# Top-32 attention with a low-rank mixer: the later replacement rounds write their own tile

## The chip, the cores and the metric

The kernel runs on one core of a Trainium2 chip. The time is device microseconds, the median of three runs: 1773.88 us (1771.52 to 1775.6). A profile of one execution, with a span of 1773.6 us, is the source of everything below. The engines are TensorE (PE; its weight loads are shown apart as PEld), VectorE (DVE), ScalarE (ACT), GpSimd (POOL) and SyncE (SP), which issues the transfers here.

## The reference

```python
# attention: B, H, S, D = 8, 8, 576, 64, float32
scores = scale * np.matmul(q, k.transpose(0, 1, 3, 2))
kth = np.partition(scores, -32, axis=-1)[..., -32:-32 + 1]
scores = np.where(scores >= kth, scores, -1e9)
attn = softmax(scores)                       # with 1e-9 added to the sum
x = concat_heads(np.matmul(attn, v))         # (8, 576, 512)
# mixer: U (576, 32), V (32, 576), w_ch1 (512, 2048), w_ch2 (2048, 512)
h = x.transpose(0, 2, 1) @ U @ V
u = x + h.transpose(0, 2, 1)
out = u + np.maximum(u @ w_ch1, 0) @ w_ch2
```

For each of 8 x 8 x 576 rows of 576 scores the 32nd largest has to be found; all scores below it are dropped. That search is the part that the change touches.

## The kernel before, in words

**Tiling.** Heads are worked in pairs: 8 batches with four pairs each make 32 pairs. The 576 rows of a head are cut into four chunks of 128 and a rest of 64. A step `(g, t)` takes pair `g` and row chunk `t`. For `t` from 0 to 3 it holds two tiles of 128 x 576 scores, one for each head of the pair; in the code these two are `chunks[0]` and `chunks[1]`, and such a step is called a two-chunk step in this text. For `t = 4` the two rests of 64 rows share one tile: a one-chunk step. So there are 160 steps, 128 with two chunks and 32 with one.

**One step.** `scores` (L310) has TensorE compute the scores, and ScalarE copies them from PSUM to the tile `Ssb` (L344 to L346, L327). `front` (L366) finds the threshold. VectorE's MAX8 at L385 gives the eight largest of each row. Then come three rounds (`i` = 1, 2, 3): at L395 a replacement sets the eight values just found to -3e38, and at L399 MAX8 finds the next eight. After three rounds the smallest of the last eight is the 32nd largest. A replacement is two instructions in the trace: MATCH_VALUE_LOAD takes in the eight values, MATCH_REPLACE8 runs over the 576 elements. Within a round both chunks are replaced first (chunk 1, then chunk 0), and then both maxima are taken. After the rounds GpSimd (L402, L403) and ScalarE with GpSimd (L419 to L421) push the scores below the threshold down, and ScalarE takes the exponent with the row sum (L351). `turns` transposes the weights on TensorE, or `blocks` does so with a VectorE transpose (L446) and transfers (L452, L456). `values` multiplies with v (L498, L508, L512), `mixed` does the low-rank mixer, and `mlp` the two big products (L581, L600).

**Buffers of the rounds.** The first round reads `Ssb`, which is still needed, and so writes elsewhere: to a tile with the tag `rr`. The second and third round read an `rr` tile and write a new one. The tag has three buffers in rotation. Taking the next buffer makes its writer wait until the last reader of the old content is done. The waits are set by the framework from the tiles that instructions name, on the same engine too.

**Order.** On TensorE, ScalarE, VectorE and GpSimd the instructions run in the order in which the code names them. `front` is a generator that the main loop (L701 to L807) advances piece by piece between other work. `fill` (L673) puts in matmuls of the previous batch's `mlp` by a fixed share per step, so that they run beside the search of the next batch. Only the transfer queue on SyncE is ordered by the framework. Weights arrive in pairs of 32-bit words and are converted during the first two batches (L174 to L189, `next_params`), on ScalarE, VectorE and GpSimd. The two big products of the last batch come after all searches.

Of the kernel before, what the change touches and what calls it, by code (L numbers as in the profile page):

```python
# [8 lines left out]
F32 = mybir.dt.float32  # L9
# [17 lines left out]
def kernel(  # L27
# [29 lines left out]
    B, H, S, D = q.shape  # L57
    P = 128
# [24 lines left out]
    attn = ctx.enter_context(tc.tile_pool(name="attn", bufs=2))  # L83
# [265 lines left out]
    def weigh(chunk, E, nmax, total=None):  # L349

        nc.scalar.activation(E, chunk, AF.Exp, bias=nmax, scale=SCALE, accum_out=total)  # L351

    def ways(g, t):

        if (g, t) == (NPAIR - 1, NT - 1):
            return (0,), (), (1,)
        if (g, t) == (NPAIR - 1, NT):
            return (0,), (), ()  # L360
        return (), (1,) if t < NT else (), (0,)
# [4 lines left out]
    def front(g, t):  # L366

        if t == 0:
            dens[g] = small.tile([P, 2 * NT + 1], F32, tag="den", name="den", bufs=3)
        chunks, den = S2s.pop((g, t)), dens[g]
        n = len(chunks)
        E2 = attn.tile([P, 2 * S], F32, tag="E", name="E", bufs=3)
        Es = [E2[:, c * S : (c + 1) * S] for c in range(n)]
        sums = [den[:, 2 * t + c : 2 * t + c + 1] for c in range(n)]
        probs[g, t] = E2
        curs, ms = list(chunks), [None] * n
        first = small.tile([P, 2, 8], F32, tag="first", name="first", bufs=3)  # L380
        nmax = small.tile([P, 2], F32, tag="nmax", name="nmax", bufs=4)
        order = (1, 0) if n == 2 else (0,)
        for c in order:
            ms[c] = first[:, c]
            nc.vector.max(ms[c], curs[c])  # L385
        yield
        early, pooled, gaps = ways(g, t)
        for i in range(1, TOPK // 8):
            if i == 1:
                nc.scalar.mul(nmax[:, 0:n], first[:, 0:n, 0], -SCALE)  # L390
                for c in early:
                    weigh(chunks[c], Es[c], nmax[:, c : c + 1])
            for c in order:
                nxt = attn.tile([P, S], F32, tag="rr", name="rr", bufs=3)
                nc.vector.match_replace(nxt, ms[c], curs[c], NEG)  # L395
                curs[c] = nxt
            for c in order:
                ms[c] = small.tile([P, 8], F32, tag="m8", name="m8", bufs=8)
                nc.vector.max(ms[c], curs[c])  # L399
            yield  # L400
        for c in pooled:
            nc.gpsimd.tensor_scalar(Es[c], chunks[c], ms[c][:, 7:8], NEG, ALU.is_lt, ALU.mult)  # L402
            nc.gpsimd.tensor_tensor(chunks[c], chunks[c], Es[c], ALU.add)  # L403
        for c in early:
            nc.vector.scalar_tensor_tensor(
                out=Es[c],
                in0=chunks[c],
                scalar=ms[c][:, 7:8],
                in1=Es[c],
                op0=ALU.is_ge,  # L410
                op1=ALU.mult,
                accum_out=sums[c],
            )
        if t == NT:
            del qkTs[g]
        yield
        for c in gaps:
            least = small.tile([P, 1], F32, tag="least", name="least", bufs=3)
            nc.scalar.mul(least, ms[c][:, 7:8], WIDEN)  # L419
            nc.scalar.activation(Es[c], chunks[c], AF.Relu, bias=least, scale=-WIDEN)  # L420
            nc.gpsimd.tensor_tensor(chunks[c], chunks[c], Es[c], ALU.subtract)  # L421
            yield
        ahead = pooled if shared(g, t) else ()
        for c in ahead:
            weigh(chunks[c], Es[c], nmax[:, c : c + 1], sums[c])
            yield
        for c in order:
            if c not in early and c not in ahead:
                weigh(chunks[c], Es[c], nmax[:, c : c + 1], sums[c])
        if t == NT and g != NPAIR - 1:  # L430
            nc.scalar.activation(den, den, AF.Identity, bias=eps)
        yield

    def shared(g, t):


        return t < NT and g * CH + t >= ROUNDED
# [263 lines left out]
    for n in range(STEPS + 2):  # L701
        g, t = divmod(n, CH)
        if n < STEPS:
            if t == 0 and g + 1 < NP:
                load(g + 1)
            if t == 1 and g + 1 < NP:
                ready = prep(g + 1)
            fronts[n] = front(g, t)
            next(fronts[n])
# [131 lines left out]
```

## Time and profile before

| | busy, us | share of the span | instructions |
|---|---|---|---|
| TensorE, matmul | 1669.3 | 94% | 9851 |
| VectorE | 1560.3 | 88% | 3106 |
| ScalarE | 1029.4 | 58% | 2682 |
| GpSimd | 846.8 | 48% | 591 |

| group | count | mean, ns | busy, us |
|---|---|---|---|
| L385 MAX8 on `Ssb` | 288 | 742 | 203.3 |
| L395 replacement, `Ssb` to `rr` (round one) | 288 | 742 | 211.8 |
| L395 replacement, `rr` to `rr` (rounds two and three) | 576 | 742 | 427.2 |
| L399 MAX8 on `rr` | 864 | 748 | 614.7 |

How to read it. Times are in us from the start of the span unless marked ns. A group is one line and one operation; L395 is line 395 of the kernel. "Idle before, releaser" tells how long the engine stood still ahead of the group's instructions and what ended that. The chain of waits is followed back from the last instruction: at each step to what released it, or to the instruction before it on its engine; "issue" in it is time in which an engine waited for nothing that the profile shows. Two instructions of one engine can overlap in the record[...]. Busy time is then counted once.

### The profile page before, as it was taken

The page shows a single profiled execution, that of the slowest core. Times are in us where ns is not written, and L with a number is a line of the kernel's source. Part 1 is how long each engine was busy: PE and PEld are TensorE (multiplying, and loading weights), DVE is VectorE, ACT ScalarE, POOL GpSimd, SP SyncE. Part 2 cuts the span into 40 slices and gives each one's busy share as a digit, 9 for nine tenths or more (in the row PEclk, how much of TensorE's full clock was granted, in tenths as well). Part 3 has the DMA queues.
Part 4 walks back from the last instruction along what each step waited for, and adds up shares of the span by engine and source line. Part 5 has one row for each costly group of instructions (what it writes and reads, how often), then busy time and mean ns, then how long its engine had stood idle before and what let it go on. Part 6 is the DMA issues. An engine that isn't in the chain of part 4 may idle for free.

```text
span 1773.6 us, 28992 instructions
## 1 busy us (share of the span) xinstructions
PE 1669.3 (94%) x9851; PEld 1257.5 (71%) x9851; DVE 1560.3 (88%) x3106; ACT 1029.4 (58%) x2682; POOL 846.8 (48%) x591
## 2 busy tenths in 40 slices
PE   4666789999999999999999999999999999999999
PEld 2434556677777877788777877788777877788677
DVE  7999989899999999999999999999999999994000
ACT  4778777555656656565656656565656656564100
POOL 4777677535354554545445454444445444453000
PEclk7687799999999999999999999999999999999999
DMA  3222332222223332222233232232233232211010
GB/s 95 88 82 73 88 85 61 50 59 71 58 67 80 66 72 56 67 68 64 64 71 79 62 70 62 65 70 63 63 73 80 59 73 60 53 50 45 4 15 13
DMA packets 275829, 112.79 MB, mean 64 GB/s; under 512 B 173920, under 2 KB 260192, under 8 KB 275680
## 3 DMA queue, kind: packets, MB, share of 16 engines
q1 hardware_dynamic: 274624, 110.68, 26.4%
q8 instruction: 77, 1.26, 0.3%
q14 instruction: 72, 0.59, 0.1%
q10 hardware_dynamic: 1056, 0.26, 0.1%
HBM read 74.15 MB, written 36.70 MB: 63 GB/s over the span
## 4 chain that ended last, share of the span: by engine, by line
PE 75%; DVE 16%; POOL 4%; ACT 3%; issue 2%; DMA 1%; SPq 0%; POOLq 0%; DVEq 0%
PE mm L581 25%; PE mm L600 24%; DVE rr L395 7%; PE sc L333 6%; PE O L512 6%; DVE m L399 6%; PE tp L474 3%; DVE first L385 2%; PE sc L320 2%; PE O L498 2%; PE up L556 1%; PE O L508 1%; POOL E L402 1%; PE up L558 1%; PE tp L648 1%
## 5 line engine op out<-in xcount | busy, mean ns | idle before, releaser
L399 DVE MAX8 m<-rr 128x8 f32<-128x576 f32 x864 | 614.7, 748 | 5.5
L600 PE MATMUL mm<-hT,w 128*128 128x256 f32 (+1 forms) x2048 | 547.4, 410 | 0.0
L581 PE MATMUL mm<-uT,w 128*128 128x256 f32 (+1 forms) x2048 | 541.5, 410 | 0.9 <-ACT hT L593 0.9
L402 POOL TENSOR_SCALAR E<-Ssb,m 128x576 f32<-128x576 f32 x127 | 281.1, 2214 | 411.7 <-DVE m L399 409.1
L581 PEld LDWEIGHTS mm<-uT,w 128*128 128x128 f32 x2048 | 371.7, 190 | 115.1 <-issue 26.0
L600 PEld LDWEIGHTS mm<-hT,w 128*128 128x128 f32 x2048 | 368.3, 190 | 106.8 <-issue 22.5
L395 DVE MATCH_REPLACE8 rr<-m,rr 128x576 f32<-128x576 f32 x576 | 427.2, 742 | 0.0
L421 POOL TENSOR_TENSOR Ssb<-Ssb,E 128x576 f32<-128x576 f32 x159 | 225.4, 1418 | 122.3 <-ACT E L420 121.7
L351 ACT ACTIVATE E<-Ssb,nmax 128x576 f32<-128x576 f32 x288 | 223.3, 776 | 52.4 <-POOL Ssb L403 34.9
L593 ACT ACTIVATE hT<-mm 128x320 f32<-128x320 f32 (+1 forms) x256 | 105.1, 411 | 240.4 <-PE mm L581 240.1
L385 DVE MAX8 first<-Ssb 128x8 f32<-128x576 f32 x288 | 203.3, 742 | 31.4 <-ACT Ssb L346 31.4
L395 DVE MATCH_REPLACE8 rr<-first,Ssb 128x576 f32<-128x576 f32 x288 | 211.8, 742 | 0.0
L403 POOL TENSOR_TENSOR Ssb<-Ssb,E 128x576 f32<-128x576 f32 x127 | 179.3, 1412 | 10.6
L333 PE MATMUL sc<-qkT 64*128 64x288 f32 x1024 | 170.6, 454 | 6.7 <-ACT Ssb L344 5.8
L474 PE MATMUL tp<-ident,E 128*128 128x128 f32 x736 | 116.0, 283 | 37.1 <-ACT XT L521 14.6
L512 PE MATMUL O<-PT,va 128*64 128x128 f32 x2048 | 146.3, 284 | 1.9 <-DMA PT<-away 1.9
L474 PEld LDWEIGHTS tp<-ident,E 128*128 128x128 f32 x736 | 92.1, 145 | 68.7 <-ACT XT L521 16.6
L475 ACT COPY PT<-tp 128x512 f32<-128x512 f32 x184 | 106.6, 585 | 49.0 <-PE tp L474 46.4
L512 PEld LDWEIGHTS O<-PT,va 128*64 128x64 f32 x2048 | 113.7, 140 | 19.0 <-DMA PT<-away 2.9
L420 ACT ACTIVATE E<-Ssb,least 128x576 f32<-128x576 f32 x159 | 123.3, 776 | 5.2
L333 PEld LDWEIGHTS sc<-qkT 64*128 64x128 f32 x1024 | 93.3, 198 | 45.3 <-issue 14.3
L613 DVE TENSOR_TENSOR oT<-uT,mm 128x320 f32<-128x320 f32 (+1 forms) x8 | 3.6, 455 | 137.1 <-PE mm L600 137.1
(81 smaller groups left out, 1574.0 us busy)
## 6 DMA issues: line engine op xcount, KB each, us to landing
away<-y SPq DMA_DIRECT2D x416, 64.0 KB, 1.8
PT<-away SPq DMA_DIRECT2D x104, 256.0 KB, 2.8
raw<-in_moe_w_ch_dram SPq DMA_DIRECT2D x32, 512.0 KB, 3.8
va<-in_v_dram SPq DMA_DIRECT2D x64, 128.0 KB, 2.3
out_dram<-ob SPq DMA_DIRECT2D x57, 128.0 KB, 2.2
ld<-in_q_dram SPq DMA_DIRECT2D x108, 64.0 KB, 2.4
ld<-in_k_dram SPq DMA_DIRECT2D x108, 64.0 KB, 2.4
ld<-in_q_dram SPq DMA_DIRECT2D x108, 8.0 KB, 2.2
```

The lines of the kernel that those rows point to most:

```text
L333: nc.tensor.matmul(sc[:, h, 0:HALF], lhsT=qkT[half(h), 0, cols(t)], rhs=qkT[half(h), 1, i * HALF : (i + 1) * HALF], start=True, stop=True,)
L351: nc.scalar.activation(E, chunk, AF.Exp, bias=nmax, scale=SCALE, accum_out=total)
L385: nc.vector.max(ms[c], curs[c])
L395: nc.vector.match_replace(nxt, ms[c], curs[c], NEG)
L399: nc.vector.max(ms[c], curs[c])
L402: nc.gpsimd.tensor_scalar(Es[c], chunks[c], ms[c][:, 7:8], NEG, ALU.is_lt, ALU.mult)
L403: nc.gpsimd.tensor_tensor(chunks[c], chunks[c], Es[c], ALU.add)
L421: nc.gpsimd.tensor_tensor(chunks[c], chunks[c], Es[c], ALU.subtract)
L474: nc.tensor.transpose(tp[:, j, :], E2[:, a : a + P], ident)
L512: nc.tensor.matmul(O[half(h)], lhsT=va[:, h, j, :], rhs=PB[:, j] if h and shared(g, t) else PT[:, NT * h + j], start=False, stop=(j == NT ...
L581: nc.tensor.matmul(ph[:, 0:w], lhsT=w1[:, cc, f * P : (f + 1) * P], rhs=uT[:, cc, lo:hi], start=(cc == 0), stop=(cc == NC - 1),)
L600: nc.tensor.matmul(po[:, 0:w], lhsT=w2[:, f, c * P : (c + 1) * P], rhs=hTs[f][:, 0:w], start=(f == 0), stop=(f == NF - 1),)
```

## The change

The second and third round no longer take a new `rr` tile; they write into the tile that they read. The first round takes a tile as before. The tag keeps its three buffers; a two-chunk step now takes two of them instead of six. The purpose is to use fewer buffers, so that a replacement doesn't have to wait for a buffer to come free.

```diff
             for c in order:
-                nxt = attn.tile([P, S], F32, tag="rr", name="rr", bufs=3)
+
+                nxt = attn.tile([P, S], F32, tag="rr", name="rr", bufs=3) if i == 1 else curs[c]
                 nc.vector.match_replace(nxt, ms[c], curs[c], NEG)
                 curs[c] = nxt
```

The added empty line moves the numbers of all later lines up by one: L395 becomes L396, L399 becomes L400.

## The prediction

> **What bounds the kernel now.** I read the page by slices first, because an average over the span mixes a beginning and a long middle. The two rows to compare are TensorE (PE) and VectorE (DVE); I leave out the rows between and after them.
>
> ```profile
> PE   4666789999999999999999999999999999999999
> ...
> DVE  7999989899999999999999999999999999994000
> ```
>
> A slice is 44.3 us. TensorE is idle a third to a half of the first four slices and full from the seventh on; VectorE is full from the second slice to 1618 us and then has nothing to do. So there are at least three stages. The next view is the busy time of each engine in stretches; I cut it where the chain of waits (below) changes its engine.
>
> ```profile
> core 0: us, PE busy (x) PEld busy (x) DVE busy (x) ACT busy (x) POOL busy (x), PEclk, DMA share, GB/s
> 0.00:165.80 165.80, 95.10 (x586) 61.97 (x586) 154.36 (x316) 116.37 (x281) 110.32 (x95) 0.78 0.31 87
> 165.80:260.90 95.10, 78.11 (x443) 52.81 (x444) 89.53 (x183) 72.18 (x172) 69.06 (x48) 0.85 0.30 81
> 260.90:445.00 184.10, 173.29 (x1045) 130.71 (x1043) 173.18 (x346) 115.36 (x301) 101.69 (x71) 0.98 0.26 62
> 445.00:1618.00 1173.00, 1172.36 (x7115) 892.85 (x7114) 1135.65 (x2249) 703.15 (x1875) 561.13 (x373) 1.00 0.29 66
> 1618.00:1773.60 155.60, 150.48 (x669) 119.18 (x667) 7.52 (x17) 22.37 (x56) 4.63 (x5) 1.00 0.07 15
> ```
>
> The fourth line decides most. In 1173 us TensorE is idle 0.6 us and VectorE 37 us. The list of waits gives VectorE 17.4 us at L385 there, waiting for the score copy of L346, and gives TensorE no wait at all. A busy TensorE is not proof of a full one, so I looked at its pace. In the chain, 16 matmuls of 320 columns take 4.31 to 4.50 us (0.27 us each) and 20 of 256 columns take 4.32 us (0.216 us each). After 1645 us, where TensorE is alone, 128 of each take 34.45 and 27.63 us, so 0.269 and 0.216 us. It is the same pace: in the middle TensorE runs as fast as it ever does, and VectorE waits for it.
>
> The chain of waits says the same. Three pieces of it, from the beginning, from the middle and the last stretch (columns: start, duration, what):
>
> ```profile
> 63.43 0.74 DVE rr L395
> 64.17 0.02 issue
> 64.19 0.82 DVE rr L395 x2
> ...
> 1115.58 1.02 PE O L512 x16
> 1116.61 1.17 PE sc L333 x8
> 1117.78 3.43 PE mm L600 x12
> ...
> 1714.10 27.63 PE mm L581 x128
> 1741.73 27.64 PE mm L600 x128
> ```
>
> From 11.3 to 165.8 us the chain is VectorE in every piece (L385, L395, L399, L186) but for issue time. From 165.8 to 260.9 us it goes through GpSimd (POOL L402, L403, L421, L187, L189), ScalarE and TensorE, with no VectorE work. From 260.9 to about 445 us VectorE stretches alternate with GpSimd, ScalarE, TensorE and transfers. From 445 us to the end it is TensorE, apart from a short handover near 1634 us.
>
> The last view is VectorE's timeline over one step with two chunks. Columns are start, duration, line, operation.
>
> ```profile
> 702.34 0.08 DVE L395 MATCH_VALUE_LOAD rr<-first,Ssb 128x8 f32 x1
> 702.40 0.75 DVE L395 MATCH_REPLACE8 rr<-first,Ssb 128x576 f32<-128x576 f32 x1
> 703.06 0.08 DVE L395 MATCH_VALUE_LOAD rr<-first,Ssb 128x8 f32 x1
> 703.12 0.74 DVE L395 MATCH_REPLACE8 rr<-first,Ssb 128x576 f32<-128x576 f32 x1
> 703.78 1.41 DVE L399 MAX8 m<-rr 128x8 f32<-128x576 f32 x2
> 705.11 0.08 DVE L395 MATCH_VALUE_LOAD rr<-m,rr 128x8 f32 x1
> 705.17 0.75 DVE L395 MATCH_REPLACE8 rr<-m,rr 128x576 f32<-128x576 f32 x1
> 705.95 0.09 DVE L395 MATCH_VALUE_LOAD rr<-m,rr 128x8 f32 x1
> 706.03 0.74 DVE L395 MATCH_REPLACE8 rr<-m,rr 128x576 f32<-128x576 f32 x1
> 706.69 1.41 DVE L399 MAX8 m<-rr 128x8 f32<-128x576 f32 x2
> ```
>
> In the first round the second value load starts 0.66 us after the first replacement began, 0.09 us before that one's end at 703.15. In the second round it starts at 705.95, after the end at 705.92. So in the first round neighbouring instructions overlap; in the second something holds the second chunk until the first chunk's replacement has ended. From value load to the next MAX8 the first round takes 703.78 - 702.34 = 1.44 us, the second 706.69 - 705.11 = 1.58 us. At 60 us the same three figures are 1.45, 1.58 and 1.57. I take 0.125 us as the price of that hold, and it occurs in rounds two and three.
>
> [...]
>
> **The change, part by part.** The tag rr has three buffers. Before, a two-chunk step takes six of them: chunk 1 writes A and chunk 0 writes B in round one; in round two chunk 1 goes from A into C, and chunk 0 from B into the oldest, A, which chunk 1's replacement, directly in front, is still reading. In round three chunk 1 goes into B and chunk 0 into C, again what the instruction in front reads. That is the hold in both rounds.
> - Removed: the two holds. In place, chunk 0 writes B, which the instruction in front doesn't touch. What it still has to wait for is its own MAX8, two instructions back, as in round one. There are 128 two-chunk steps (32 head pairs with four each), so 256 holds, 256 x 0.125 = 32 us of VectorE time. One-chunk steps have each instruction waiting on the one in front through the data, before and after: nothing there.
> - Added: in the built program the first MAX8 of rounds two and three now has a wait of its own on the replacement of its chunk; before, that had been covered by the hold. That replacement lies two instructions back and ended 0.6 us before, as in round one, where such a wait sits and MAX8 follows its replacement after 0.66 us. Queued behind it are the other MAX8 and the next round; nobody waits. Cost nothing.
> - Reading and writing the same 576 elements: no replacement in the trace does this. Lower bound nothing: L186 works in place (w<-w) on 512 elements in 0.41 us at 63 us. Upper bound 0.25 us per round, if the two replacements stayed serial and a MAX8 also had to stop. I take nothing, because L186 shows no price for it, and keep the upper end for the slower rival.
> - Moved: the order of work on TensorE is the same, on VectorE, ScalarE and GpSimd too (only buffers have other names). In the transfer queue, which isn't ordered by hand, a few loads change places with the transfers of L452 by one or two positions. The queue waits for L446 345.7 us in all, 103 times, so it is early; TensorE waits for PT<-away 1.9 us in the whole run. Nothing.
>
> What lies on the path: up to 165.8 us there are 16 steps, three of them one-chunk, so 13 x 2 = 26 holds, 26 x 0.125 = 3.25 us. They count in full: the scores of the next step lie ready some 9 us ahead (L346 ends at 119.7 us, its L385 starts at 128.5 us), and the GpSimd chain that follows is started by a VectorE result, after GpSimd had been idle 3.5 us. From 165.8 to 260.9 us: nothing. From 260.9 to 445 us I count 17 holds in the chain, 2.1 us. TensorE has 184.1 - 173.3 = 10.8 us of idle time to give up there, but other waits (GpSimd, transfers) are close behind, so I take two thirds, 1.4 us. After 445 us: nothing, since TensorE's queue is full; VectorE's 23 us there (92 two-chunk steps x 0.25) turn into longer waits at L385. The tail starts from TensorE's own last filler: nothing. Sum 3.25 + 1.4 = 4.65 us, so 1773.9 - 4.7 = 1769.2 us.
>
> **Rivals.**
> - The gain is absorbed in the beginning: from 165 us GpSimd and ScalarE set the pace, and if one of them is limited earlier by its own queue (ScalarE is busy 116 of 165.8 us, GpSimd 110), less than 1 us is left. For: they take over the chain at 165.8. Against: before it they wait for VectorE (ScalarE 2.8 us at L419 for m, at 117.5 and again at 165.8 us). Time 1773 to 1774 us.
> - VectorE is the bound all the way: 32 us fewer, 1742 us. For: 97% busy in the middle. Against: TensorE's 0.6 us of idle time in 1173 us.
> - Slower: in-place replacements bring a new stop, net one more of 0.125 us per round. In the middle 23 us more just fill VectorE's waits of 17.4 + 6.0 us, but the 43 holds on the path turn from gain to loss: 1773.9 + 5.4 = 1779 us. For: the operation isn't in the trace. Against: round one has the same distances and no stop.
>
> **How the numbers follow.** Forecast 0.71 (1768.5 if all 43 holds count, 1770.6 if only the first 26 do), absorbed 0.15, VectorE all the way 0.04, slower 0.10. The range takes the forecast and the absorbed case with about 1.5 us for the measurement (the three runs of before lie 4 us apart) and leaves out the two ends: 1766.0 to 1774.2 us. Faster by over 0.2% means below 1770.3: most of the forecast case and all of the third, 0.64. Within 0.2%: the rest of the forecast and the absorbed case, 0.26. Slower: 0.10.
>
> **What would show it.** Right: in rounds two and three the second value load 0.66 us behind the first replacement; VectorE busy some 30 us less or idle more; its waits at L385 after 445 us up from 17 us to about 40; step 16 beginning some 3 us before 166 us; the chain still TensorE from about 440 us; TensorE's idle time before 445 us smaller by the gain. Wrong: replacements longer than 0.75 us, a MAX8 that starts late, a TensorE that was not full in the middle, or GpSimd taking the chain earlier than 165 us.

## The result, and the profile after

The changed kernel takes 1766.22 us (median of four runs, 1765.58 to 1767.12), the kernel before in the same group 1773.36 us (1771.52 to 1775.6). The ratio is 0.996, with a 95% interval from 0.9942 to 0.9977. The gain is 7.1 us by the medians, where 4.7 were forecast; the interval reaches from 4 to 10 us, so this group alone doesn't tell the two apart. In the two later groups (below) it was 8.4 us with four buffers and 8.8 us for the changed kernel again (interval of the ratio 0.9935 to 0.9968, so at least 5.7 us). The ratios need not be exactly the quotients of the medians. The two profiled executions lie 8.5 us apart (spans 1773.6 and 1765.1 us), and the accounts below are of that pair. The one of the kernel before took 1775.4 us, near the upper end of its runs.

First VectorE's timeline over the same step as the one shown of before. Line 395 is now 396, line 399 is 400.

```profile
693.59 0.07 DVE L396 MATCH_VALUE_LOAD rr<-first,Ssb 128x8 f32 x1
693.65 0.74 DVE L396 MATCH_REPLACE8 rr<-first,Ssb 128x576 f32<-128x576 f32 x1
694.31 0.08 DVE L396 MATCH_VALUE_LOAD rr<-first,Ssb 128x8 f32 x1
694.38 0.74 DVE L396 MATCH_REPLACE8 rr<-first,Ssb 128x576 f32<-128x576 f32 x1
695.03 1.41 DVE L400 MAX8 m<-rr 128x8 f32<-128x576 f32 x2
696.36 0.07 DVE L396 MATCH_VALUE_LOAD rr<-m,rr 128x8 f32 x1
696.42 0.74 DVE L396 MATCH_REPLACE8 rr<-m,rr 128x576 f32<-128x576 f32 x1
697.08 0.08 DVE L396 MATCH_VALUE_LOAD rr<-m,rr 128x8 f32 x1
697.15 0.74 DVE L396 MATCH_REPLACE8 rr<-m,rr 128x576 f32<-128x576 f32 x1
697.81 1.41 DVE L400 MAX8 m<-rr 128x8 f32<-128x576 f32 x2
```

The hold is gone. In round two the second value load starts 697.08 - 696.42 = 0.66 us behind the first replacement, while that is still running (it ends at 697.16). From value load to MAX8 the round takes 697.81 - 696.36 = 1.45 us, where it was 1.58. A replacement in place takes 0.74 us, as one from tile to tile did, and the MAX8, which now has a wait of its own, follows after 0.66 us. What the prediction said of the single round holds.

Next the stretches of the span, cut at the same times as before (columns as there). The same work lies up to 8.5 us earlier in them.

```profile
core 0: us, PE busy (x) PEld busy (x) DVE busy (x) ACT busy (x) POOL busy (x), PEclk, DMA share, GB/s
0.00:165.80 165.80, 101.03 (x586) 66.56 (x586) 155.39 (x320) 118.20 (x287) 111.97 (x97) 0.74 0.30 87
165.80:260.90 95.10, 78.58 (x448) 52.99 (x448) 89.22 (x184) 72.25 (x171) 67.64 (x47) 0.86 0.30 84
260.90:445.00 184.10, 175.94 (x1076) 133.03 (x1077) 174.39 (x353) 117.11 (x307) 103.15 (x71) 0.99 0.26 62
445.00:1618.00 1173.00, 1172.41 (x7129) 894.89 (x7128) 1114.26 (x2237) 700.17 (x1874) 561.17 (x375) 1.00 0.28 66
```

In the middle TensorE is as full as before (1172.41 of 1173 us, it was 1172.36), and VectorE works 21.4 us less (1114.26, it was 1135.65). Where did that time go? The list of VectorE's waits for 445 to 1618 us:

```profile
DVE first L385 <- ACT Ssb L346: 23.7, 29, 1.2
DVE y L447 <- ACT E L351: 19.9, 17, 1.3
DVE den L488 <- ACT den L432: 6.5, 1, 6.5
```

The same list for the kernel before has two lines:

```profile
DVE first L385 <- ACT Ssb L346: 17.4, 24, 1.0
DVE y L446 <- ACT E L351: 6.0, 9, 0.7
```

VectorE's saved time became waiting, mostly at the transpose of L447 and at L488. The wait at L385 grew to 23.7 us, not to the 40 us that the prediction named. Over the whole run VectorE is busy 20.0 us less (1560.3 and 1540.3 us), not 30: part of each hold was idle time (0.03 us at 705.92 in the kernel before, by estimate 8 us for 256 holds), and L186, the shift of the weights' conversion, is busy longer (below).

To see where the end time came from, I compare when the same step begins in both profiles: the start of its first MAX8 (L385); for steps 60 and 90 the start of ScalarE's L390, one for each step. How much earlier it begins is called the lead below.

| step | before, us | after, us | earlier by | forecast |
|---|---|---|---|---|
| 16 | 165.99 | 163.81 | 2.18 | 3.25 |
| 25 | 260.87 | 258.52 | 2.35 | 3.25 |
| 30 | 315.90 | 313.02 | 2.88 | |
| 44 | 460.28 | 453.70 | 6.58 | 4.65 |
| 45 | 468.26 | 460.69 | 7.57 | 4.65 |
| 60 | 626.85 | 618.87 | 7.98 | 4.65 |
| 90 | 927.21 | 918.75 | 8.46 | 4.65 |
| end of the span | 1773.6 | 1765.1 | 8.5 | 4.65 |

From step 70 on the lead stays at 8.5 us. All of it but 0.9 us is made by step 45, in the main as forecast. Its parts have other sizes: less in the first stage, three times the forecast in the third (4.2 us from step 25 to 44, forecast 1.4), and 1.9 us after it where nothing was expected.

How exact is a lead? Of the 2.18 us at step 16, 0.14 us are there at step 0, ahead of the first replacement, so the first stage gave 2.04 us. In seven profiles without holds in that stage it lies between 2.03 and 2.09 us. Later it scatters more: late_only (below) is the kernel before up to step 47, and its profile is 0.04 us behind that of before at step 16 and 0.96 us ahead at step 44.

### The profile page after: what moved, and what is told of

Its sections match the earlier page's. It is cut to its first block, busy times and chain, and to the rows that moved or that the text cites. A ratio compares the mean times of both kernels' runs of the same rounds, so it can differ in the third digit from the quotient of the medians.

```text
span 1765.1 us, 28989 instructions
## 1 busy us (share of the span) xinstructions
PE 1670.0 (95%) x9851; PEld 1259.5 (71%) x9851; DVE 1540.3 (87%) x3106; ACT 1026.2 (58%) x2682; POOL 846.4 (48%) x591
## 3 DMA queue, kind: packets, MB, share of 16 engines
q8 instruction: 77, 1.26, 0.3%
## 4 chain that ended last, share of the span: by engine, by line
PE 78%; DVE 13%; POOL 4%; ACT 3%; issue 1%; DMA 1%; SPq 0%; POOLq 0%; DVEq 0%
PE mm L582 26%; PE mm L601 25%; PE sc L333 7%; PE O L513 6%; DVE rr L396 6%; DVE m L400 5%; PE tp L475 3%; DVE first L385 2%; PE sc L320 2%; PE O L499 2%; PE up L557 1%; PE O L509 1%; POOL E L403 1%; PE up L559 1%; PE tp L649 1%
## 5 line engine op out<-in xcount | busy, mean ns | idle before, releaser
L400 DVE MAX8 m<-rr 128x8 f32<-128x576 f32 x864 | 614.3, 747 | 5.5
L403 POOL TENSOR_SCALAR E<-Ssb,m 128x576 f32<-128x576 f32 x127 | 280.9, 2212 | 366.2 <-DVE m L400 346.1
L396 DVE MATCH_REPLACE8 rr<-m,rr 128x576 f32<-128x576 f32 x576 | 423.2, 741 | 0.0
L385 DVE MAX8 first<-Ssb 128x8 f32<-128x576 f32 x288 | 203.7, 743 | 38.5 <-ACT Ssb L346 37.8
L396 DVE MATCH_REPLACE8 rr<-first,Ssb 128x576 f32<-128x576 f32 x288 | 211.7, 742 | 0.0
L333 PE MATMUL sc<-qkT 64*128 64x288 f32 x1024 | 170.7, 454 | 6.3 <-ACT Ssb L344 5.2
L421 ACT ACTIVATE E<-Ssb,least 128x576 f32<-128x576 f32 x159 | 123.3, 776 | 5.2
L333 PEld LDWEIGHTS sc<-qkT 64*128 64x128 f32 x1024 | 93.2, 197 | 44.6 <-issue 14.0
```

Source lines behind the costliest of these rows:

```text
L333: nc.tensor.matmul(sc[:, h, 0:HALF], lhsT=qkT[half(h), 0, cols(t)], rhs=qkT[half(h), 1, i * HALF : (i + 1) * HALF], start=True, stop=True,)
```

## Experiments

Theory: chunk 0's replacement waited for the instruction in front of it, because it took the tile that this one was reading; that cost 0.125 us twice a step, and it shortens the run only while TensorE is not full. Rivals: working in place helps by itself, VectorE counts all the way, or the order of the transfers brings the gain.

**No hold, nothing in place.** All rounds take new tiles, from four buffers.

```diff
-                nxt = attn.tile([P, S], F32, tag="rr", name="rr", bufs=3)
+                nxt = attn.tile([P, S], F32, tag="rr", name="rr", bufs=4)
...
-    HT = 10
+    HT = 9
```

> Nothing is done in place; every round takes a new rr tile as before, but the tag has four buffers instead of three, so that chunk 0's replacement doesn't take the tile that the instruction in front reads. To find the room, the tag hT has nine buffers instead of ten. Theory (the hold on the instruction in front was the cost): as fast as the in-place kernel, 1766 us, with 0.66 us from the first replacement to the second value load in all rounds. Rival (in place itself helps, through fewer tiles or less traffic on the buffers): as before, 1773 us.

Measured: 1766.84 us (1766.11 to 1767.0), before 1775.25 us in this group, ratio 0.9949 (0.9937 to 0.9962). VectorE's timeline in this kernel, rounds one and two of a step:

```profile
60.25 0.08 DVE L395 MATCH_VALUE_LOAD rr<-first,Ssb 128x8 f32 x1
...
62.62 0.09 DVE L395 MATCH_VALUE_LOAD rr<-m,rr 128x8 f32 x1
62.69 0.75 DVE L395 MATCH_REPLACE8 rr<-m,rr 128x576 f32<-128x576 f32 x1
63.35 0.09 DVE L395 MATCH_VALUE_LOAD rr<-m,rr 128x8 f32 x1
```

Again 0.66 us (62.69 to 63.35), and the whole gain. In place is one way to be rid of the hold, a fourth buffer is another; in place by itself brings nothing that shows.

**Half a dose.** Round two in place, round three into a new tile.

```diff
+                nxt = attn.tile([P, S], F32, tag="rr", name="rr", bufs=3) if i != 2 else curs[c]
```

> Round two in place, round three into a new tile: one of the two holds of a step is left, the one of round three. Theory (each hold costs about 0.125 us and they add up): half of the gain, 1769.5 to 1770 us, and the second value load 0.66 us behind the first replacement in round two, 0.78 us in round three. Rival (it is the waits of the MAX8 or the rotation that matter): near one of the ends, 1766 or 1773 us.

Measured: 1769.18 us (1767.98 to 1770.11), ratio 0.9962 (0.9948 to 0.9976): 6.1 us by the medians, nearly three quarters of the 8.4 us that this group gave without holds, and a little more than expected. Its timeline shows a round of each kind, the second with the hold:

```profile
62.83 0.75 DVE L395 MATCH_REPLACE8 rr<-m,rr 128x576 f32<-128x576 f32 x1
63.49 0.08 DVE L395 MATCH_VALUE_LOAD rr<-m,rr 128x8 f32 x1
...
65.60 0.75 DVE L395 MATCH_REPLACE8 rr<-m,rr 128x576 f32<-128x576 f32 x1
66.39 0.09 DVE L395 MATCH_VALUE_LOAD rr<-m,rr 128x8 f32 x1
```

The distance is 0.66 us in round two and 0.79 us in round three, so 0.13 us for one hold. From step to step the lead grows by half: 1.03 us in the first stage, where 2.04 us came without holds, and 3.1 us at step 44, where it was 6.6. What follows, 1.1 us from step 44 to 45 and another 1.1 us up to the end, is about as large as with the whole change; that is why the time moved by more than half. This part doesn't go by the holds (more on it below).

**Where in the run.** In place in the first 48 steps only, then in the others only.

```diff
+                nxt = attn.tile(...) if i == 1 or g * CH + t >= 48 else curs[c]   # early_only
...
+                nxt = attn.tile(...) if i == 1 or g * CH + t < 48 else curs[c]    # late_only
```

> In place in steps 0 to 47 only (up to about 490 us), new tiles afterwards. Theory (the gain comes from the stages in which TensorE still has idle time, and in the middle TensorE is full): nearly the whole gain, 1766 to 1768 us. Rival (VectorE counts all the way): 48 of 160 steps, so about 2 us of the 7 us, 1771 us.

> New tiles in steps 0 to 47, in place from step 48 on: the other part of the change alone. Theory: no gain but for the two waits of TensorE for PT<-away at steps 49 and 69, 0.9 us in all: 1772.5 to 1773.5 us. Rival (VectorE counts all the way): 112 of 160 steps, 5 us, 1768 us. Rival (the order of the transfers brings it): a gain here too, of more than 1 us.

Measured: early_only 1766.92 us (1766.36 to 1767.16), ratio 0.995 (0.9937 to 0.9962), the whole gain from 48 of the 160 steps. late_only 1774.2 us (1772.33 to 1775.73), ratio 0.9999 (0.9991 to 1.0007), no gain that shows from the other 112 (1.05 us by the medians, at most 1.6 us by the interval), although it too takes VectorE's work in the long middle down. The rival of the whole way falls: late_only should have had 5 us.

The rival of the transfers isn't settled by this pair. The order of the transfers in the changed kernel differs from that of before from 114 us on, early_only and four_buffers have the changed order too, and late_only keeps the old one up to 470 us. But round_two_only keeps the old order up to 329 us and has that of the changed kernel from 336 to 430 us. In both stretches its two-chunk steps gain 0.12 to 0.14 us each where the holds count, half of the 0.25 us without holds. So the gain that comes step by step goes by the holds and not by the order of the transfers.

**VectorE relieved of much more in the middle.** From step 48 on the third round is left out.

```diff
         for i in range(1, TOPK // 8):
+            if i == 3 and g * CH + t >= 48:
+                yield
+                continue
```

> The changed kernel itself, as the measure for the others of this group: 1766 us, 7 to 8 us under the kernel before. Its first MAX8 of step 44 some 6.5 us and of step 16 some 2.2 us earlier than before.

> In place as changed; from step 48 on the third round is left out (its replacement and its MAX8), so that the threshold there is the 24th largest value. This takes 2.8 us of VectorE's work from each of some 90 two-chunk steps, eight times what the change takes from all of them. Theory (TensorE is full in the middle): 1765.5 to 1766.5 us, no gain over the changed kernel. Rival (VectorE counts all the way): some 200 us less. Between the two: a few us, if TensorE has hidden waits on VectorE in the middle.

Measured: the changed kernel 1765.95 us (1765.65 to 1766.89), ratio to before 0.9951 (0.9935 to 0.9968); with the round left out 1766.64 us (1765.83 to 1767.26). The stretch from 445 to 1618 us of the latter, and VectorE's waits in it:

```profile
445.00:1618.00 1173.00, 1172.41 (x7126) 894.37 (x7125) 843.37 (x1632) 696.35 (x1874) 561.66 (x374) 1.00 0.29 66
...
DVE first L385 <- ACT Ssb L346: 220.2, 89, 5.2
DVE first L385 <- ACT Ssb L327: 48.8, 23, 2.7
DVE y L450 <- ACT E L351: 43.9, 38, 1.9
```

VectorE has 271 us less to do there (843.37, after 1114.26) and TensorE the same 1172.41 us. The time doesn't move beyond the scatter. That VectorE was 97% busy in this stretch said nothing on what it is worth there.

**Why the first stage gave 2.0 and not 3.25 us.** From step to step the lead over the kernel before grows by 0.25 us, but five two-chunk steps of the thirteen add nothing (3, 6, 8, 11, 13). In each of them stands an L186 that takes 0.23 to 0.26 us longer than before. For step 13, VectorE and GpSimd in the kernel before:

```profile
142.34 1.41 POOL L403 TENSOR_TENSOR Ssb<-Ssb,E 128x576 f32<-128x576 f32 x1
142.88 1.14 DVE L186 TENSOR_SCALAR w<-w 128x512 uint32<-128x512 uint32 x1
```

and in the changed kernel:

```profile
140.67 1.40 POOL L404 TENSOR_TENSOR Ssb<-Ssb,E 128x576 f32<-128x576 f32 x1
140.96 1.39 DVE L186 TENSOR_SCALAR w<-w 128x512 uint32<-128x512 uint32 x1
```

L186 takes 0.41 us with GpSimd idle (at 111.28 us in the kernel before). Here it ends 0.27 us behind GpSimd's instruction before (144.02 and 143.75) and 0.28 us after (142.35 and 142.07), though it starts earlier after the change. In the kernel before it ends 0.27 to 0.29 us behind L403, L421 or L189 in all 12 places where one of them is running when it starts on `w`, and takes 0.49 to 1.61 us there. Beside the comparison L402, which was also first, it doesn't wait:

```profile
131.32 2.26 POOL L402 TENSOR_SCALAR E<-Ssb,m 128x576 f32<-128x576 f32 x1
...
132.65 0.41 DVE L186 TENSOR_SCALAR w<-w 128x512 uint32<-128x512 uint32 x1
```

So the wait is measured; why it comes behind some of GpSimd's instructions and not behind L402, no view shows. GpSimd's instruction in step 13 moved by 1.67 us, VectorE's own lead was 1.92 us, and the difference of 0.25 us was lost in the wait. Two kernels without L186 test whether it is L186 that loses it.

```diff
-        nc.vector.tensor_single_scalar(bits, bits, 3, ALU.logical_shift_left)
```

> The kernel before without L186, the bit shift on VectorE in the conversion of the weights, so that the weights it works with are not those of the reference. L186 is the only instruction of VectorE that was seen to stretch when GpSimd is busy. It is the measure for the next run.

> The changed kernel without L186. Theory (each of the 13 two-chunk steps before 166 us gains 0.25 us, and where L186 waits for GpSimd it gives that back): step 16 begins 3.2 us earlier than in the kernel before without L186, where with L186 it was 2.2 us; no step gains nothing. Rival (the five steps without a gain have another reason, such as the replacements): about 2.2 us here too.

Measured: 1757.14 us (two runs) and 1751.06 us (two runs). The first MAX8 of step 16 begins at 157.15 and at 153.56 us, 3.59 us apart, of which 0.25 us are there at step 0 already. So 3.34 us in 13 steps, 0.257 us each, and every one of them adds its share. The first stage's term was right but for the wait of L186. From step 23 on the lead of this pair goes up and down (4.7 us at step 22, 2.8 at 35, 4.8 at 44); I didn't follow that.

**Using VectorE's slack.** With VectorE faster, more filler matmuls might fit into the steps up to 42.

```diff
-    SLOTS, SHORT, EARLY = 8, 0.65, 0.91
+    SLOTS, SHORT, EARLY = 8, 0.65, 0.95   # fill_095; 1.0 in fill_100
```

> In place as changed, and the share of filler matmuls in the first 42 steps is raised from 0.91 to 0.95 (EARLY), since VectorE now has a little to spare there. Theory: TensorE's idle time between 215 and 445 us shrinks, 1764 to 1766 us. Rival: the scores come later, VectorE waits longer, and the first stage loses it again: 1767 us or more.

> In place as changed, and that share at 1.0. If more filler helps, 1763 to 1766 us; if 0.91 was near its best for the faster VectorE too, slower than the changed kernel by up to 3 us.

Measured: 1764.89 us (1764.31 to 1765.69) with 0.95 and 1766.62 us (1764.55 to 1767.01) with 1.0, where the changed kernel had 1765.95 us (1765.65 to 1766.89) in the same group. 0.95 is the fastest version that was run with the whole computation, 1.1 us under the changed kernel; the runs of the two just touch, so the step is small and not much beyond the scatter. 1.0 gains nothing.

## Why the prediction was right, point by point

The mechanism and the place were right; that the time fell inside the stated range has luck in it. 1766.22 us lies 0.2 us above its lower end of 1766.0, and the same kernel took 1765.95 us in the later group.

- **The hold, its cause and its price: right.** 0.125 us was taken from the rounds' lengths; one hold measures 0.13 us in round_two_only, 0.257 us for two in the pair without L186. That it is the buffer and not the work in place is shown by four_buffers.
- **Nothing for reading and writing the same tile, nothing for the new wait of MAX8: right.** 0.74 us and 0.66 us, as in round one.
- **TensorE is full from 445 us on, so nothing is to be had there: right in the main**, shown by late_only and above all by middle_two_rounds. The step "after 445 us: nothing" missed 0.9 us at two places, steps 49 and 69. There the kernel before has TensorE's multiplication with PT, the transposed weights, stretched (step 69):

```profile
714.79 1.57 PE L512 MATMUL O<-PT,va 128*64 128x128 f32 x16
```

and the changed kernel has not:

```profile
706.81 1.09 PE L513 MATMUL O<-PT,va 128*64 128x128 f32 x16
```

  Half a microsecond is missing between matmuls of one group, and the list of waits doesn't show it. The chain of before has the transfer PT<-away from 712.36 to 715.23 us and behind it 14 of the 16 matmuls, so it probably came late for them. The prediction used the list's 1.9 us for this transfer as all there was. That the change cured this isn't shown: other profiles have such a group at other steps, the second one of the changed kernel too (1.23 us at 806.96 us).
- **First stage 3.25 us: 1.2 us too much.** The failed half-sentence is "They count in full". The ready scores and the idle GpSimd were looked at, the wait of L186 on GpSimd was not, though L186 takes 1.14 us in the kernel before at 142.88 us. The chain up to 165.8 us also holds some 0.8 us of ScalarE (L345, L346, L419), which changes nothing here.
- **Third stage: the term that was mis-sized.** "Other waits (GpSimd, transfers) are close behind, so I take two thirds, 1.4 us." From step 25 to 44 came 4.2 us. Two-chunk steps that added 0.25 to 0.27 us each make up 3.6 us of it: steps 25 and 26, and all twelve from step 30 to 43. Steps 27 to 29, where VectorE waits 5.4 us for the scores afterwards, together added nothing. So those waits took nothing away in 14 of 16 two-chunk steps. Counting the holds on the chain gave 17 in the stage. But the chain is one path: it leaves VectorE where an answer goes out and comes back later, and holds in between don't show though they also delay what follows. The lead from step to step is the better count.
- **The other 0.6 us of that stage is not from holds.** It came from step 34, which has one chunk, to step 35. TensorE's granted clock is 0.50 there for 6.8 us in the kernel before and for 3.4 us in the changed one (from 362.4 and 360.4 us). late_only, with the same code as before up to there, has about half as much of it as the kernel before (0.78 on average from 362.5 to 369.5 us, where the kernel before has 0.52) and gains 0.4 us; four_buffers, without holds, has about as much as the kernel before by its matmuls (8 of L333 take 2.29 us in both, 1.24 us some 10 us later) and loses 0.4 us. So this part goes with the clock of the single execution.
- **A jump of 1.0 us from step 44 to 45: not foreseen.** TensorE in the kernel before, around 445 us (start, duration, and in brackets the idle time ahead):

```profile
443.69 0.44 PE L648 MATMUL tp<-ident,oT 128*128 128x128 f32 x2 [1.92 <-POOL oT L616]
...
445.44 1.98 PE L512 MATMUL O<-PT,va 128*64 128x128 f32 x16
```

and in the changed kernel:

```profile
437.61 0.44 PE L649 MATMUL tp<-ident,oT 128*128 128x128 f32 x2 [1.51 <-POOL oT L617]
...
438.93 1.09 PE L513 MATMUL O<-PT,va 128*64 128x128 f32 x16
```

  Before, the same 16 matmuls take nearly twice as long: the granted clock is half for 3.4 us (0.50 from 444.35 to 447.76 us, and so 0.61 on average from 445.0 to 448.5 us; 1.00 in the changed kernel at the same work, from 437.5 to 441.0 us). Half speed for 3.4 us where TensorE is the bound costs 1.7 us by estimate; the lead shows 1.0 us of it. The four other profiles without holds up to there (the changed kernel again, four_buffers, early_only, middle_two_rounds) jump by 0.8 to 1.0 us and round_two_only by 1.1 us, all at full clock (1.00 from 430 to 450 us); late_only has the half clock (0.52 from 444 to 446 us) and loses 0.1 us. So the jump goes with the clock; whether the change brings it is left open below.
- **Absorbed, VectorE all the way, slower: all three rivals fell**, the first because 7 to 8 us are there, the second by late_only, the third by the timeline.

The size was off by errors of both signs, -1.2 us in the first stage and +2.8 and +1.9 us behind it. Step by step the holds account for 5.6 us of the 8.5 (2.0 in the first and 3.6 in the third stage); the 0.6, 1.0 and 0.9 us that came on top have not been shown to be theirs.

## What to carry to other kernels

When tiles rotate through a few buffers, look which instruction last read the buffer that the next writer gets: if it was the one directly in front on the same engine, the two did not overlap here (0.78 us from the first replacement to the second value load, at 705.17 us in the kernel before), and both writing in place and one more buffer gave that back (0.66 us). What such a saving is worth has to be read stage by stage; in the stage where TensorE was full (busy 1172.41 of 1173 us), even 271 us of VectorE's work taken away changed nothing (1766.64 us, after 1765.95). To size it, compare when the same step begins in two profiles, rather than count pieces on the chain of waits.

## What was not expected of the hardware

- A wait on the instruction directly in front cost 0.13 us on VectorE at 576 elements (0.79 us from the first replacement to the second value load in round three of round_two_only, 0.66 us in its round two), although the order of the two was the same without it; a wait on the instruction one further back cost nothing that shows (0.66 us from start to start in round one, which has such waits).
- L186 on VectorE (512 elements, 0.41 us alone) took up to 1.6 us (at 242.88 us in the kernel before) behind L403, L421 and L189 on GpSimd and ended 0.27 to 0.29 us behind them; beside L402 it took 0.41 us (at 132.65 us). Leaving it out took 17 us off the kernel before (1774.3 to 1757.14 us, few runs), the largest gain seen here; it isn't a version of this kernel as it stands.
- The half clock near 445 us came after long pauses, but not after all of them. TensorE paused 1.92 us in the kernel before and 1.80 us in late_only, and both had it (0.59 and 0.52 from 444 to 446 us); it paused 1.26 to 1.79 us in the changed kernel (both profiles), four_buffers, early_only, round_two_only and middle_two_rounds, and none had it there (1.00 from 430 to 450 us). But the length alone doesn't decide here: before_no_shift paused 1.90 us at the same place and kept the full clock (1.00 from 260.9 to 445 us; the 16 matmuls take 1.09 us).

```profile
425.97 0.44 PE L647 MATMUL tp<-ident,oT 128*128 128x128 f32 x2 [1.90 <-POOL oT L615]
...
427.29 1.09 PE L511 MATMUL O<-PT,va 128*64 128x128 f32 x16
```

  And fill_095 had a half clock (0.50 from 436 to 438 us) after pauses of 1.66 us (before 429.29 us) and 1.67 us (before 434.18 us). Between 215 and 1760 us the half intervals of the two kernels compared last 3.41 us (from 444.35 us before and from 360.42 us after) and 6.83 us (from 362.43 us before). It is one profile for each kernel (two of the changed one), so what sets the half clock here stays open, and with it whether the change also saved clock.
